# A new issue order for a fused attention and gated-convolution kernel, with q and k of the first batch loaded in alternating halves

## The chip, the cores and the metric

The kernel runs on one core of a Trainium2 chip. The metric is device time in microseconds for one launch. The core has five engines that work from queues of their own, each in order: PE (matrix products into PSUM, eight banks), DVE and ACT (both read PSUM and write SBUF), POOL (elementwise work in SBUF, and the issue of the input loads) and SP (the issue of transposing copies inside SBUF and of the stores). PEld is the loading of weights for PE.

## What is computed

For 8 batches, 8 heads, 576 positions and 64 dimensions a head: attention with an exponential feature map of 2 x 128 features, then a gated convolution over the positions, done with a real Fourier transform of length 576, and a projection out.

```python
def phi(x):
    proj = np.einsum('bhsd,df->bhsf', x, w_phi)
    proj = proj - np.max(np.abs(proj), axis=-1, keepdims=True)
    return np.concatenate([np.exp(proj), np.exp(-proj)], axis=-1)
q_p, k_p = (phi(q), phi(k))
kv = np.einsum('bhsf,bhsd->bhfd', k_p, v)
z = np.sum(k_p, axis=2)
num = np.einsum('bhsf,bhfd->bhsd', q_p, kv)
den = np.einsum('bhsf,bhf->bhs', q_p, z)[..., None] + 1e-06
x = num / den                                   # heads put side by side: 8 x 576 x 512
x1, x2, x3 = np.split(x @ w_proj, 3, axis=-1)
X2 = np.fft.rfft(x2, n=S, axis=1)
H = np.fft.rfft(filter_fft, n=S, axis=0)[None, :, :]
y = x1 * np.fft.irfft(X2 * H, n=S, axis=1) * x3
out = y @ w_out
```

## The kernel before

The program is a table of small steps, the methods of one class, and a text `PLAN` of some 1,480 words that says in which order they are issued. A word is a method with its arguments and, behind an @, the first PSUM bank that it uses: `Pk,0,1@4` is the k projection of batch 0, pair of heads 1, into banks 4 and 5. `run` (L1026) goes through the words from first to last. Each engine takes its own instructions in that order; between engines only data, PSUM banks and the buffers of rings (two, three or four deep, the dictionary `RING`) hold them back. So the order of the words, the banks and the engine named in a word are the schedule.

One batch goes like this; v is a pair of heads (0 to 3), X a half of the heads (0 or 1), m or c a block of 128 columns or rows.

- Loads by POOL: `load` (L554), 576 KB, or `loadh` (L560), one half of it. q and k are then transposed, by SP with `trh` (L566) or, for batch 0, by PE with `pt`, whose result ACT or DVE copies out (`pte`).
- `Pk`, `Qn`, `Pkt`, `Qnt` (L591 to L621) project with `w_phi` on PE; `maxk`, `maxq` and the short `maxkt`, `maxqt` take the absolute maxima on DVE; `ex`, `exkt`, `exqt` are the exponentials on ACT. `Pq` with `Pqt` projects q once more, with the maxima, transposed through `trm`, subtracted in PSUM. `em` and `vs` scale v by the exponential of k's maxima (ACT, then POOL or DVE).
- `KV` and `NE` with `NEt` (L736) are the attention products on PE; `rc`, `xn`, `rct`, `xnt` divide on DVE. The result is x. It is transposed by SP with `trx` (L780) and `trxt`, or by PE with `ptx` (L789) and `ptxt` and a copy.
- `f1` and `f2` (POOL or DVE) fold x, `F` transforms it (PE), `X2` projects the transform with `w_proj`, `Y1` and `m3` multiply by the filter's transform.
- `X1` and `X3` project the transposed x (in the helper `proj`, whose matmuls are L884), `tm` multiplies them; `I` transforms back (for some blocks cut in two steps, `It` and `Is`), `Ie`, `Ip`, `Im` and `ym` (L1002, POOL or DVE) combine; for one block of four, in most batches, `J` and `yj` do it in one.
- `O` multiplies by `w_out` (L1014), `Oe` copies out, `st` (L1020) stores. A block of 128 rows in pairs of batches (`O,b,4`, with `yt`) takes the remainders of two batches.

At the start the kernel also builds the Fourier matrices: `gi_part`, `gi_fr`, `gi_nr` (POOL) make index tables, `cols_f`, `cols_i` (DVE) factors from them, `ang` (ACT or DVE) angles, `frac` (DVE) reduces them, `sin` (ACT) is the sine. The filter comes with `fl_load` (eight pieces) and `fl_loadt` on SP's queue; `fa` (POOL, L491) folds it, `Hd` transforms it on PE, `He` copies it out. `wz` (L312) is two products of zeros on PE whose result nobody reads; `w_load` loads the other weights.

The batches overlap: while PE projects batch b out, batches b+1 to b+3 are in their attention or loading. The plan fixes how they interleave.

Of the kernel before, what the change touches and what calls it, by code (L numbers as in the profile page):

```python
# [1076 lines left out]
```

## Time and profile before

| | us |
|---|---|
| median of 3 runs | 303.11 |
| lowest and highest of them | 302.89, 308.19 |
| the profiled execution, whole | 304.44 |
| its span, first to last instruction | 302.7 |
| PE busy in the span | 275.4 |
| DVE, ACT, POOL busy | 260.4, 225.8, 208.8 |

All times below are from the one profiled execution, in microseconds from the start of its span. A row of the timeline has its start, its length, the engine and line, the operation with output and input, and in brackets the idle time ahead of it with what ended that. Rows of stretches give the busy time of PE, PEld, DVE, ACT and POOL, then the granted PE clock as a share of full speed, the DMA engines' share and GB/s. Rows of waits give the waiting line, what it waited for, and then the sum, the number and the longest of such waits.

### The profile page before, as it was taken

What the parts mean: (1) busy time and instruction counts of PE and PEld (TensorE: products, weight loads), DVE (VectorE), ACT (ScalarE), POOL (GpSimd) and SP (SyncE); (2) the same over time, 40 slices, a digit from 0 to 9 for tenths busy, and PEclk for the clock granted to TensorE, in tenths of its full rate; (3) what the DMA queues carried; (4) which work ended last, traced back from release to release, by engine and by line L of the source; (5) the groups of instructions that cost most, each with busy time, mean ns of one, the idle gap of its engine ahead of it and who ended that gap; (6) DMA issues with size and microseconds to landing.
All of it is one profiled execution on the core that took longest, in us unless ns stands there. A gap on an engine that the chain in (4) does not pass through costs nothing.

```text
span 302.7 us, 10174 instructions
## 1 busy us (share of the span) xinstructions
PE 275.4 (91%) x4287; PEld 201.3 (67%) x4316; DVE 260.4 (86%) x440; ACT 225.8 (75%) x361; POOL 208.8 (69%) x168
## 2 busy tenths in 40 slices
PE   1858689999999999998999969999999999999992
PEld 0627563778667876686768757667588767786761
DVE  8998779799989799989899976789989998887773
ACT  7999887798868887685988657987758997932320
POOL 8119594997985768469998639968768759443550
PEclk9978899999999999999999999999999999999999
DMA  7999999997999859997998966997734342040426
GB/s 135 191 191 185 186 205 170 159 160 119 107 159 202 117 114 155 175 176 119 200 167 151 106 111 106 155 194 118 132 76 69 71 89 64 20 98 2 90 63 196
DMA packets 72446, 40.12 MB, mean 133 GB/s; under 512 B 52752, under 2 KB 67216, under 8 KB 72400
## 3 DMA queue, kind: packets, MB, share of 16 engines
q1 hardware_dynamic: 57184, 22.56, 43.6%
q0 software_dynamic: 14816, 16.25, 35.3%
q8 instruction: 33, 0.54, 0.8%
q10 hardware_dynamic: 400, 0.66, 0.8%
q14 instruction: 13, 0.11, 0.1%
HBM read 33.75 MB, written 9.44 MB: 143 GB/s over the span
## 4 chain that ended last, share of the span: by engine, by line
PE 72%; ACT 9%; DVE 8%; DMA 5%; issue 3%; POOL 2%; SPq 0%; DVEq 0%; ACTq 0%
PE ps L884 17%; PE ps L862 12%; PE ps L1014 9%; PE ps L729 5%; PE ps L937 5%; PE ps L743 4%; DMA xT<-xn 3%; PE ps L603 2%; PE ps L630 2%; DVE mq L672 2%; PE ps L893 2%; PE ps L827 2%; PE ps L596 2%; PE ps L823 2%; PE ps L636 2%
## 5 line engine op out<-in xcount | busy, mean ns | idle before, releaser
L884 PE MATMUL ps<-xT,wproj 128*128 128x256 bf16 x512 | 64.2, 273 | 3.4 <-DMA xT<-xn 3.3
L884 PEld LDWEIGHTS <-wproj 128*128 128x128 bf16 x512 | 48.3, 98 | 13.6 <-issue 4.1
L672 DVE TENSOR_REDUCE mq<-ps 128x8 f32<-128x1024 f32 (+1 forms) x40 | 43.7, 1112 | 5.2 <-PE ps L603 2.5
L672 DVE TENSOR_REDUCE mk<-ps 128x8 f32<-128x1024 f32 (+1 forms) x40 | 44.2, 1112 | 4.6 <-PE ps L596 3.3
L1003 POOL TENSOR_TENSOR yT<-cv,x1s 128x576 bf16<-128x576 f32 x24 | 30.8, 1298 | 18.2 <-DVE x1s L929 9.5
L817 POOL TENSOR_TENSOR xf<-SD 128x512 bf16<-128x512 bf16 x25 | 29.1, 1177 | 14.3 <-DVE SD L811 13.7
L876 POOL TENSOR_TENSOR T<-T,T 128x1024 bf16<-128x1024 bf16 x14 | 29.6, 2122 | 13.2 <-DVE T L872 13.2
L714 POOL TENSOR_TENSOR vp<-vn,vp 128x1152 bf16<-128x1152 bf16 x14 | 30.2, 2154 | 9.0 <-ACT vp L708 9.0
L658 ACT ACTIVATE Eqp<-ps 128x1024 bf16<-128x1024 f32 x32 | 32.6, 1040 | 4.8 <-PE ps L636 4.8
L658 ACT ACTIVATE Eqm<-ps 128x1024 bf16<-128x1024 f32 x32 | 32.7, 1041 | 4.6 <-PE ps L636 4.6
L714 POOL TENSOR_TENSOR vm<-vn,vm 128x1152 bf16<-128x1152 bf16 x16 | 35.1, 2197 | 1.0 <-ACT vm L708 0.7
L658 ACT ACTIVATE Ekp<-ps 128x1024 bf16<-128x1024 f32 x32 | 33.0, 1035 | 2.9 <-PE ps L596 1.9
L1014 PE MATMUL ps<-wout,yT 128*128 128x512 bf16 x132 | 34.1, 380 | 0.9 <-POOL xf L817 0.2
L658 ACT ACTIVATE Ekm<-ps 128x1024 bf16<-128x1024 f32 x32 | 33.1, 1036 | 1.4 <-DVE mk L672 0.9
L862 PE MATMUL ps<-wproj,XF 128*128 128x512 bf16 x119 | 30.0, 380 | 0.6 <-issue 0.2
L811 POOL TENSOR_TENSOR SD<-xn 128x512 bf16<-128x512 bf16 x20 | 23.0, 1171 | 9.2 <-DVE xn L762 7.8
L296 ACT CAST x1s<-ps 128x512 bf16<-128x512 f32 (+1 forms) x32 | 17.9, 560 | 14.9 <-PE ps L884 7.9
L958 DVE TENSOR_TENSOR cv<-es,ps 128x288 f32<-128x288 f32 x52 | 21.2, 445 | 4.0 <-PE ps L862 1.4
L925 DVE TENSOR_TENSOR x1s<-ps,x1s 128x512 bf16<-128x512 f32 x32 | 21.8, 683 | 3.0 <-PE ps L884 2.1
L762 DVE TENSOR_TENSOR xn<-ps,r 128x512 bf16<-128x512 f32 x32 | 21.8, 688 | 1.0
L743 PE MATMUL ps<-KVs,Eqp 128*128 128x65 bf16 x256 | 20.5, 195 | 1.7 <-ACT Eqp L658 0.9
L1014 PEld LDWEIGHTS <-yT 128*128 128x128 bf16 x144 | 12.9, 98 | 13.5 <-POOL yT L1003 0.8
(177 smaller groups left out, 673.5 us busy)
## 6 DMA issues: line engine op xcount, KB each, us to landing
out_dram<-o SPq DMA_DIRECT2D x67, 128.0 KB, 2.6
vn<-in_v_dram POOLq DMA_DIRECT2D x8, 576.0 KB, 6.9
kn<-in_k_dram POOLq DMA_DIRECT2D x7, 576.0 KB, 8.5
qn<-in_q_dram POOLq DMA_DIRECT2D x7, 576.0 KB, 9.6
wproj<-in_moe_w_proj_dram POOLq DMA_DIRECT2D x3, 512.0 KB, 9.8
fl<-in_moe_filter_fft_dram SPq DMA_DIRECT2D x8, 128.0 KB, 6.8
out_dram<-o ACTq DMA_DIRECT2D x5, 128.0 KB, 2.8
...
```

Of the source, the lines that this page charges most:

```text
L658: self.nc.scalar.activation(e, p, AF.Exp, bias=0.0, scale=1.0 if g == "p" else -1.0)
L672: self.nc.vector.tensor_reduce(out=out, in_=src, axis=AX.X, op=ALU.max, apply_absolute_value=True)
L714: self.eng(eng).tensor_tensor(out=t[:, :, :, 0:64], in0=self.at("vn", b)[:, 2 * X:2 * X + 2], in1=t[:, :, :, 64:65].to_broadcast([128, 2, ...
L743: self.mm(self.pb(u, 65 * a, 65 * a + 65), E, KVs[:, u, v, s, :], start=(s == 0), stop=(s == 1))
L762: self.nc.vector.tensor_tensor(out=o, in0=n[:, :, :, 0:64], in1=self.at("r", 4 * b + v).to_broadcast([128, 2, 4, 64]), op=ALU.mult)
L811: self.eng(eng).tensor_tensor(out=o[:, :, 2 * i:2 * i + 2, :], in0=x[:, :, 0:2, :], in1=x[:, :, 2:4, :], op=ALU.subtract if i else ALU.add)
L817: self.eng(eng).tensor_tensor(out=o[:, :, 2 * i:2 * i + 2, :], in0=x[:, :, 0:4:2, :], in1=x[:, :, 1:4:2, :], op=ALU.subtract if i else ALU ...
L862: self.mm(self.pb(0), l, w[:, kt, 512:1024], start=(kt == 0), stop=(kt == 3))
L876: self.eng(eng).tensor_tensor(out=Y, in0=Y, in1=self.at(f"T{2 * e + 1}", b), op=ALU.add)
L884: self.mm(o[:, d], w[:, kt, f0 + 128 * m:f0 + 128 * m + 128], y[:, 1, ::-1, ::-1] if d else y[:, 0], start=(kt == 0), stop=(kt == 3))
L1003: self.eng(eng).tensor_tensor(out=self.at("yT", b)[:, m, 0:SEQ], in0=self.turn_of("cv", (b, m)).rearrange("p x h t -> p (x h t)"), in1=sel ...
L1014: self.mm(self.pb(0), y[:, kt, 128 * c:128 * c + 128], w[:, kt, :], start=(kt == 0), stop=(kt == 3))
```

## The change

Only the text `PLAN` differs; every method is as before. The words are almost the same multiset: 1,484 for 1,483. What differs in kind:

- At the start POOL issues the first halves of q and k, then the second halves (before: q, q, k, k, with the generators in between at other places), then `load,q,1`, `load,v,0`, `load,k,1` (before: `load,k,1`, `load,q,1`, `load,v,0`). The first `loadh` stands ahead of `gi_part`. One of the three first filter loads is put later; four of the other pieces stand between `trh,q,1,0` and `trh,q,1,1`, three behind `trh,k,1,1`.
- `ang,3` goes to ACT and `ang,4` to DVE; one copy `pte` goes from ACT to DVE, `ptxe` of batch 0 wholly to DVE, `gen_neg` to ACT. Eight `wz` instead of nine, with other places and banks.
- `trxt,0` on SP replaces `ptxt,0` on PE; `ptx,3,3` on PE replaces `trx,3,3` on SP; `It` and `Is` replace two `I`.
- Many evacuations (`X1e`, `Fe`, `KVe`, `Oe`, `f1`, `f2`, `m3`, `trme`) change between ACT, DVE and POOL; one `ym` of the last batch goes from POOL to DVE.
- The order of the words, and the banks, differ throughout: `load,q,3` stands ahead of `ym,POOL,0,0`; `trh,q,4,1` stands ahead of `trx,2,0`; `load,q,7` stands behind `load,k,7`.

The lines of the plan in which these stand, out of 163 removed and 163 added:

```diff
-fl_load,2,0 cols_m gi_part fl_load,1,1 loadh,q,0,0 cols_f fl_load,2,1 gi_fr w_load,phi cols_i
-loadh,q,0,1 ang,ACT,1 gi_nr loadh,k,0,1 ang,ACT,4 ang,DVE,3 loadh,k,0,0 load,k,1 ang,ACT,0 gz,DVE
-ident wz,18@0 frac,3 load,q,1 wz,2@1 load,v,0 frac,1 ang,DVE,2 pt,q,0,0,0@0 sin,3 w_phi zeros
...
-ex,k,m,0,3@2 Pq,0,1@6 trh,k,1,1 exkt,m,0@0 w_load,proj,0 Pq,0,3@2 em,p,0,1 em,m,0,1 ex,q,p,0,1@6
-vs,POOL,m,0,1 Qn,1,0@0 fl_loadt KV,0,0@4 ex,q,m,0,1@6 maxq,1,0@0 fl_load,0,1 fl_load,0,0
-ex,q,m,0,3@2 Pq,0,2@6 fl_load,1,0 KVe,DVE,0,0@4 Pk,1,1@0 ex,q,m,0,2@6 vs,POOL,p,0,1 fl_load,3,1
...
-fa,POOL,1 ptx,0,2@7 rc,0,0@0 ex,k,p,1,0@4 NEt,0@2 xn,0,0@0 rct,0@2 ptxe,ACT,0,2@7 ptx,0,0@6
-xnt,0,1@2 ptx,0,3@4 xnt,0,0@2 Pk,1,3@0 ptxe,ACT,0,3@4 ptxe,DVE,0,0@6 fa,POOL,0 Pkt,1@2 Qn,1,2@6
...
-He,ACT,4,0@1 F,0,3@4 vs,POOL,m,1,0 tm,0,3@0 F,0,1@6 Fe,ACT,0,3@4 ptxt,0@1 F,0,0@2 trh,q,2,0
...
-Pq,1,3@4 em,p,2,0 rc,1,1@6 xn,1,1@6 KV,1,1@2 load,q,3 ex,q,m,1,3@4 Im,0,2@0 trx,1,1 vs,POOL,p,2,0
...
-X3,1,3@3 rc,2,0@6 exkt,p,3@4 rc,2,1@0 xn,2,0@6 exkt,m,3@4 X1,1,0@2 xn,2,1@0 trx,2,0 tm,1,3@3
-f1,POOL,2,0,0 Pqt,2@0 maxkt,3@4 KV,2,1@6 trx,2,1 exqt,p,2@0 m3,POOL,1,0 exqt,m,2@0 Pq,2,3@4
...
-F,2,0@0 st,SP,0,2,1 yt,ACT,1 O,1,0@6 ex,k,m,3,0@2 f1,DVE,2,1,0 st,SP,0,0,0 Fe,DVE,2,0@0 trh,q,4,1
...
-X1t,2@1 trx,3,3 Im,2,3@2 J,2,0@6 Ip,2,3@2 X1te,ACT,2@1 tmt,2@0 st,SP,1,2,1 Im,2,2@4 ym,POOL,2,3
...
-ym,POOL,3,1 maxk,5,1@2 exqt,p,4@6 J,3,2@0 st,SP,2,1,1 Ie,3,0@4 st,SP,2,3,1 Im,3,0@4 load,q,7
...
-I,7,1@6 tmt,7@0 tm,7,1@5 Ie,7,1@6 I,7,0@2 ym,POOL,7,3 Ip,7,1@6 Ie,7,0@2 X3,7,2@5 Im,7,1@6
-ym,POOL,7,1 Ip,7,0@2 J,7,2@6 Im,7,0@2 tm,7,2@5 ym,POOL,7,0 O,6,3@2 yj,7,2@6 Oe,ACT,6,3@2 yt,DVE,7
-O,7,1@6 st,SP,6,3,1 O,7,4@7 Oe,ACT,7,1@6 st,SP,6,3,0 O,7,3@2 st,ACT,7,1,0 st,SP,7,1,1 Oe,DVE,7,4@7
-O,7,2@6 st,ACT,7,4,1 st,SP,7,4,0 Oe,DVE,7,3@2 O,7,0@7 st,ACT,7,3,0 st,SP,7,3,1 Oe,DVE,7,2@6
-st,ACT,7,2,1 st,SP,7,2,0 Oe,DVE,7,0@7 st,ACT,7,0,1 st,SP,7,0,0
+fl_load,2,1 cols_m loadh,q,0,0 fl_load,1,1 w_load,phi gi_part gi_fr cols_f loadh,k,0,0 cols_i
+ang,ACT,0 gi_nr ang,ACT,1 loadh,q,0,1 loadh,k,0,1 ang,DVE,4 load,q,1 ang,ACT,3 gz,DVE ident wz,18@0
+load,v,0 one frac,1 pt,q,0,0,1@1 ang,DVE,2 load,k,1 pt,q,0,0,0@0 pte,DVE,q,0,0,1@1 sin,1 frac,3
+wz,2@1 pte,DVE,q,0,0,0@0 pt,k,0,0,0@2 w_phi frac,0 Qn,0,0@0 frac,2 sin,0 Qn,0,1@4 pt,q,0,1,0@3
+sin,3 maxq,0,1@4 pt,k,0,1,1@6 pt,q,0,1,1@7 pte,DVE,q,0,1,0@3 sin,2 maxq,0,0@0 Qn,0,2@4
+pte,ACT,q,0,1,1@7 wz,23@3 pt,k,0,1,0@7 maxq,0,2@4 pt,k,0,0,1@3 pte,ACT,k,0,1,0@7 wz,9@0
...
+maxq,0,3@0 Qnt,0@6 ex,k,m,0,0@4 fl_load,1,0 fl_load,3,1 ex,k,p,0,0@4 maxk,0,1@2 Pk,0,2@0
+fl_load,0,0 ex,k,p,0,2@0 fl_loadt maxqt,0@6 trh,q,1,1 maxk,0,0@4 ex,k,m,0,2@0 Pkt,0@6 ex,k,m,0,1@2
...
+trh,k,1,0 maxk,0,3@4 mhi,0 exkt,m,0@6 wz,28@1 mlo,DVE,0 ex,k,m,0,3@4 vs,DVE,p,0,0 trm,0@0 wz,26@6
...
+em,m,0,1 ex,q,p,0,3@2 Pk,1,1@4 Qn,1,3@0 w_load,proj,1 maxk,1,1@4 ex,q,m,0,3@2 vs,POOL,m,0,1
+KVe,DVE,0,0@6 ex,k,m,1,1@4 Pq,0,2@2 maxq,1,3@0 NE,0,1@6 ex,q,m,0,2@2 w_load,proj,2 rc,0,1@6
+KV,0,1@0 ex,q,p,0,2@2 xn,0,1@6 gen_ends,POOL trx,0,1 ex,k,p,1,1@4 Pq,0,0@2 KVe,DVE,0,1@0 Pk,1,0@6
+ex,q,m,0,0@2 fa,POOL,1 maxk,1,0@6 NE,0,3@0 NE,0,2@4 ex,q,p,0,0@2 rc,0,3@0 xn,0,3@0 ex,k,m,1,0@6
+Pqt,0@2 rc,0,2@4 NE,0,0@0 fa,POOL,0 xn,0,2@4 exqt,p,0@2 rc,0,0@0 exqt,m,0@2 wz,22@4 xn,0,0@0
+ptx,0,2@5 ex,k,p,1,0@6 ptx,0,3@4 ptxe,DVE,0,2@5 Qnt,1@0 NEt,0@2 ptxe,DVE,0,3@4 load,v,1 maxqt,1@0
...
+Hd,0@6 maxq,1,1@2 ex,k,p,1,2@0 X3,0,3@4 trxt,0 vs,POOL,m,1,0 He,ACT,0,0@6 He,DVE,4,0@7 F,0,3@0
...
+em,p,2,0 exkt,m,2@2 I,0,0@0 rc,1,0@4 exkt,p,2@2 xn,1,0@4 NE,1,1@6 Ie,0,0@0 load,q,3 I,0,1@2 trx,1,0
...
+f1,DVE,2,0,1 f1,POOL,2,0,0 Pk,3,1@6 exqt,p,2@0 trh,q,4,1 X3,1,0@4 maxk,3,1@6 exqt,m,2@0
+ex,q,m,2,3@2 NE,2,2@0 f2,POOL,2,0,1 trx,2,0 tm,1,0@4 X2,1,4@5 ex,q,p,2,3@2 rc,2,2@0 xn,2,2@0
...
+tmt,2@1 st,SP,1,1,1 Ip,2,3@4 I,2,2@6 Im,2,3@4 trh,k,5,1 Ie,2,2@6 ptx,3,3@1 ym,POOL,2,3 I,2,1@4
...
+X1e,ACT,4,2@4 X3,4,3@5 X1e,DVE,4,3@2 load,k,7 ex,k,m,5,3@0 f1,DVE,4,1,1 O,3,3@2 load,q,7 rct,4@6
...
+ym,DVE,7,1 X3,7,0@0 st,SP,6,0,1 Im,7,3@6 st,SP,6,2,0 X1,7,2@4 Oe,DVE,6,1@1 ym,POOL,7,3 tm,7,0@0
+X3,7,2@1 st,SP,6,1,0 X1e,ACT,7,2@4 Ip,7,0@2 st,SP,6,1,1 Im,7,0@2 J,7,2@6 tm,7,2@1 ym,POOL,7,0
+O,6,3@1 yj,7,2@6 Oe,ACT,6,3@1 yt,DVE,7 O,7,1@6 st,SP,6,3,1 O,7,4@7 Oe,ACT,7,1@6 st,SP,6,3,0 O,7,3@1
+st,ACT,7,1,1 st,SP,7,1,0 Oe,DVE,7,4@7 O,7,0@6 st,ACT,7,4,1 st,SP,7,4,0 Oe,DVE,7,3@1 O,7,2@7
+st,ACT,7,3,1 st,SP,7,3,0 Oe,DVE,7,0@6 st,ACT,7,0,1 st,SP,7,0,0 Oe,DVE,7,2@7 st,ACT,7,2,1
+st,SP,7,2,0
```

279 lines of the change are left out of this document (136 added, 143 removed).

## The prediction

> **What bounds the kernel now.** I read the page's first part, then the busy time by stretches, then the waits of the matmul engine in the long middle, then the timeline at the three places where it stands still.
>
> ```profile
> span 302.7 us, 10174 instructions
> ## 1 busy us (share of the span) xinstructions
> PE 275.4 (91%) x4287; PEld 201.3 (67%) x4316; DVE 260.4 (86%) x440; ACT 225.8 (75%) x361; POOL 208.8 (69%) x168
> ```
>
> PE is busy 275.4 of 302.7 us, so 27.3 us is all that an order could give back. Where these lie:
>
> ```profile
> core 0: us, PE busy (x) PEld busy (x) DVE busy (x) ACT busy (x) POOL busy (x), PEclk, DMA share, GB/s
> 0.00:10.00 10.00, 3.62 (x26) 2.10 (x28) 8.63 (x54) 8.16 (x14) 7.44 (x21) 1.00 0.86 144
> 10.00:30.00 20.00, 14.91 (x272) 10.50 (x272) 18.91 (x25) 19.78 (x30) 8.19 (x6) 0.83 1.16 190
> 30.00:40.00 10.00, 7.34 (x169) 6.32 (x164) 6.99 (x13) 7.61 (x11) 6.67 (x6) 0.83 1.26 191
> 40.00:290.00 250.00, 242.20 (x3803) 178.68 (x3824) 220.56 (x342) 189.03 (x307) 183.77 (x135) 1.00 0.78 125
> 290.00:302.70 12.70, 7.28 (x40) 3.67 (x39) 5.36 (x10) 1.17 (x2) 2.75 (x3) 0.97 0.45 125
> ```
>
> Up to 40 us PE lacks 6.4 + 5.1 + 2.7 = 14.1 us; from 10 to 30 us ACT (19.78 of 20) and DVE (18.91) are the bound there, not PE and not the loads. From 40 to 290 us PE works 242.20 of 250 and is itself the bound: 7.8 us are lost. The end loses 5.4. Of the 7.8 the trace names these:
>
> ```profile
> PE ps L884 <- DMA xT<-xn: 3.3, 2, 2.4
> PE ps L743 <- issue: 0.8, 1, 0.8
> PE ps L596 <- ACT Eqm L658: 0.6, 1, 0.6
> PE ps L611 <- DVE xnt L774: 0.4, 1, 0.4
> PE ps L603 <- DMA qT<-qn: 0.3, 1, 0.3
> ```
>
> The two at the top are projections of x that wait for a transposed x, once in batch 3 and once in batch 4:
>
> ```profile
> 141.95 1.58 PE L884 MATMUL ps<-xT,wproj 128*128 128x256 bf16 x13 [0.90 <-DMA xT<-xn]
> ...
> 176.34 2.45 PE L884 MATMUL ps<-xT,wproj 128*128 128x256 bf16 x21 [2.40 <-DMA xT<-xn]
> ```
>
> **The change, part by part.** The matmuls are the same but for trifles: one warming pair `wz` fewer, `ptx,3,3` (four transposes on PE) for `trx,3,3`, `trxt,0` for `ptxt,0` (two off PE), `It`+`Is` for two `I`. I set their sum to zero: a PE second counts only past 40 us, and there four transposes come against two. So the time can move only through waits: at the head, in the middle, at the end.
>
> *Head, start.* POOL now issues the first half of q ahead of `gi_part`, on which DVE's `cols_f` and so ACT's first `ang` wait:
>
> ```profile
> 1.40 0.88 POOL L561 DMA_DIRECT2D qn<-in_q_dram  x1 [0.23 <-issue]
> ```
>
> That issue is 0.88 us, and 0.23 of idle just ahead of it may hide part, so the generators start 0.6 to 0.9 us later; I take 0.6, since the queue's own start-up hides some too. `gi_fr` keeps one load ahead of it, as before. ACT gets `ang,3` (three wide operations) for `ang,4` (two wide), +0.6, and loses one of three transposed-input copies, -0.65:
>
> ```profile
> L420 ACT ACTIVATE turn<-fr,cols 128x288 f32<-128x288 f32 x4 | 2.2, 613 | 0.0
> ```
>
> ```profile
> L296 ACT COPY kT<-ps 128x640 bf16<-128x640 bf16 (+1 forms) x2 | 1.2, 642 | 0.0
> ```
>
> DVE takes that copy (0.44) and, with a third `maxq` of 1.2 ahead of the copy of the first k, brings that k about as late as ACT comes free; `frac,4` and one `ang` go out of its way.
>
> ```profile
> L298 DVE COPY qT<-ps 128x512 bf16<-128x512 bf16 (+1 forms) x3 | 1.3, 440 | 0.1
> ```
>
> ```profile
> L672 DVE TENSOR_REDUCE mq<-ps 128x8 f32<-128x1024 f32 x3 | 3.6, 1214 | 0.0
> ```
>
> The first exponential, now here:
>
> ```profile
> 15.32 1.02 ACT L658 ACTIVATE Ekp<-ps 128x1024 bf16<-128x1024 f32 x1
> ```
>
> comes 0.6 us later, and because ACT has next to no gaps to 30 us, it stays 0.6 later. The order of the loads itself (v of batch 0 ahead of k of batch 1, `load,q,1` earlier, four filter loads between the transposes of q and k of batch 1) I cost at nothing: no engine is short of these bytes between 10 and 30 us, ACT's and DVE's work is the cover, and if it were gone, POOL's `fa` would be the first to be late, since it waits for the last filter load now:
>
> ```profile
> POOL fs L492 <- DMA fl<-in_moe_filter_fft_dram: 3.3, 1, 3.3
> ```
>
> Behind `fa` on POOL stand `load,v,1`, `load,k,2` and the first `f1`. A wait of up to 3.3 there is what POOL bears today without PE waiting for it by name, so it adds nothing.
>
> *Head, end.* Before, the first projection follows this:
>
> ```profile
> 37.68 0.69 DVE L762 TENSOR_TENSOR xn<-ps,r 128x512 bf16<-128x512 f32 x1
> 39.37 0.21 DVE L768 RECIPROCAL rt<-ps 128x8 f32<-128x8 f32 x1 [0.99 <-PE ps L752]
> 39.61 0.86 DVE L774 TENSOR_TENSOR xnt<-ps,rt 64x256 bf16<-64x256 f32 x2
> 40.39 0.41 DVE L298 COPY xT<-ps 128x512 bf16<-128x512 bf16 x1
> ```
>
> ```profile
> 41.25 0.76 PE ps L884 x6
> ```
>
> so 2.9 us after the last `xn` of batch 0 ends (38.37). After the change `rct` and both `xnt` stand behind, and DVE makes all three copies of 0.41 and one short maximum (about half of 1.2): 1.8 us of DVE work plus the transposes' hand-over, so 2.0. Gain 0.9. The head is then 0.6 - 0.9 = -0.3. Its bounds: this stretch also holds a stall inside one group of `Pq` matmuls,
>
> ```profile
> 31.47 1.49 issue
> ```
>
> which may or may not come again (-1.8), and upwards the 0.9 of the late start with no gain at the end (+0.9).
>
> Also, one warming pair fewer (eight for nine) meets a PE whose clock falls to a half in the head:
>
> ```profile
> 20.00:22.50 2.50, 1.27 (x6) 0.57 (x5) 2.50 (x4) 2.33 (x7) 0.83 (x2) 0.50 1.01 151
> 22.50:25.00 2.50, 2.50 (x28) 1.55 (x28) 2.50 (x2) 2.50 (x7) 2.36 (x3) 0.50 1.10 209
> ```
>
> With a second such stretch of 5 us PE would do half its work in it: at most 2.5 us, less what ACT's bound hides. I put that into the upper bound of the head, +0.9 + 2.5 = +3.4, not into the sum. The Trainium skill (TensorE: Matmul & The Clock Gate, section "What's actually happening") holds that one idle window of some 3.4 us halves PE's clock and a busy one restores it; that speaks against fewer warming matmuls, and by it the time would be 302.8. The trace agrees with its half, 0.50 in both rows.
>
> *Batch 3.* `trx,3,3` leaves SP's queue; PE transposes and ACT copies (0.59, ACT is at 76% in the middle). Three SP transposes remain and the last of them hangs on an earlier `xn`; the wait of 0.90 goes. -0.9, between 0 and -0.9; what is late next there is PE itself.
>
> *Batch 4.* The transposed x landed 5.82 us after its issue, with a 576 KB load of q issued into it:
>
> ```profile
> 170.48 5.82 DMA xT<-xn
> ```
>
> ```profile
> 171.83 0.81 POOL L555 DMA_DIRECT2D qn<-in_q_dram  x1
> ```
>
> ```profile
> DMA to landing us min/median/max: 3.8/4.4/5.8
> ```
>
> That load (`load,q,7`) is moved on POOL behind two `ym` and an `f2`, so past this wait, and one of two stores between the transposes goes. With the median of the four transposes there, 4.4, the wait shrinks by 1.4; with 3.8 by 2.0, with 5.8 by nothing. I take -1.4.
>
> *Batch 3's q.* `load,q,3` moves on POOL ahead of `ym,0,0`, where POOL waits for DVE; its transposes then come earlier and the 0.3 on L603 goes: -0.3 (0 to -0.3).
>
> *End.* The last product waits for POOL:
>
> ```profile
> PEld L1014 <- POOL yT L1003: 0.5, 1, 0.5
> ```
>
> ```profile
> 288.95 3.84 POOL L1003 TENSOR_TENSOR yT<-cv,x1s 128x576 bf16<-128x576 f32 x3 [3.87 <-DVE x1s L929]
> ```
>
> Three `ym` on POOL, 1.28 each; one of them goes to DVE, so POOL is done before the last `J` and the wait goes: -0.5. The last five products, their copies and stores keep their order but for one swap.
>
> *New waits.* The changed places in SP's and POOL's queues can make a wait of the kind seen: their median in the list above is 0.6. I add one: +0.6.
>
> Sum: -0.3 - 0.9 - 1.4 - 0.3 - 0.5 + 0.6 = -2.8. The profiled execution took 304.44 us (302.7 of span, 1.74 around it), 1.3 above the median of the runs, 303.11; the difference is put on the median: **300.3 us**. With the bounds (all gains at their least, the head at +3.4 and three new waits, +5.2; all at their most, -5.5) this case by itself runs from 297.6 to 308.3.
>
> **The rivals.** *Slower: x comes late in the middle.* SP is one queue. Before, `trx,2,0` and `trx,2,1` are issued ahead of a transpose of batch 4; now `trh,q,4,1` stands ahead of all four `trx,2`, and it waits for a load of 576 KB and for the last reader of q of batch 2. Behind it on SP are the four transposes of x, and on those hang PE's projections. The `trx` of batches 1, 3 and 4 share that queue with stores and transposes in new places. If each of these four batches pays what batch 4 pays now, that is 4 x 2.4 = 9.6 in place of 3.3, +6.3: 309.4. It decides once the last transpose lands later than PE has filler, and batch 4 shows that 5.8 us is too late. For it: batches 3 and 4 wait already, so the cover is thin. Against it: batches 1 and 2 do not, and in the new order no fewer groups of matmuls stand between a batch's last `NE` and its first projection. Chance 0.24.
>
> *Faster by more.* All named waits of the middle go (5.4 in the list), and the end's 0.5, and the head's 0.3: -6.2, 296.9. For it: each is tied to a place in the order; against it: L743's 0.8 is "issue", which no order shows. Chance 0.19.
>
> *Nothing happens.* What is gained at one place is waited for at the next, PE work being equal: 303.1. Chance 0.12. That leaves 0.45 for the forecast.
>
> **How the numbers follow.** The bound of 2%, about what a measurement of this kernel can tell from no change, lies at 297.0 and 309.2. The forecast and the third rival end within it but for their edges; the faster rival lies on its edge and gets 0.19 beyond; the slower one sits at its edge with its spread upwards, 0.26 with the forecast's own tail. Within: 0.55. The range goes from 296.0 (the faster rival with a little more) to 310.0 (the slower one with one more wait); some 0.05 is left out below and 0.13 above.
>
> **What would show it.** Right: the wait of L884 on xT below 2 us in total; the first exponential near 15.9 and the first L884 near 41; PE busy within 1 us of 275.4; no wait of L1014 on POOL at the end. Wrong: a wait of L884, L596 or L603 on a DMA of over 2 us in batches 1, 2 or 5; `fs` on POOL waiting for its load longer than 3.3; PEclk at 0.5 for a stretch past 25 us; or DVE above 90% in the middle, with PE waiting for its maxima.

## The result, and the profile after

| | before | after |
|---|---|---|
| median, us | 303.0 (302.75 to 308.19) | 312.45 (311.17 to 312.9) |
| after / before | | 1.031, 95% 1.027 to 1.035 |
| span of the profiled execution | 302.7 | 308.4 |

The change is slower by 3.1%; 300.3 was forecast, with a range to 310.0. Some executions of a kernel come out in a slower state, over 1.5% above its fastest: the medians here and below are over all of them, the ratios over the others alone. The profiled execution of the changed kernel took 311.17, the least of its four.

First the page of the changed kernel, its span and its first part:

```profile
span 308.4 us, 10199 instructions
## 1 busy us (share of the span) xinstructions
PE 278.4 (90%) x4316; PEld 201.3 (65%) x4316; DVE 268.0 (87%) x446; ACT 223.2 (72%) x359; POOL 204.3 (66%) x164
```

PE is busy 3.0 longer than before (29 of its records were missing there) and idle 2.7 longer. The stretches of before, once more, for the changed kernel:

```profile
0.00:10.00 10.00, 2.26 (x12) 1.39 (x13) 7.35 (x49) 6.55 (x11) 7.24 (x21) 1.00 0.79 119
10.00:30.00 20.00, 14.14 (x232) 8.88 (x231) 17.88 (x26) 19.20 (x31) 6.38 (x5) 0.83 1.20 191
30.00:40.00 10.00, 5.84 (x152) 5.29 (x152) 7.94 (x10) 6.17 (x8) 7.89 (x6) 0.83 1.15 206
40.00:290.00 250.00, 242.83 (x3837) 177.57 (x3837) 223.57 (x344) 188.30 (x307) 179.14 (x132) 0.99 0.73 122
```

Up to 40 PE is 3.6 less busy than before (2.26 + 14.14 + 5.84 = 22.2 for 25.9), so the head is late by about that. In the long middle PE is as busy as before, but at a clock of 0.99, and the waits are others. PE's waits, and two groups of the page:

```profile
PE ps L743 <- DVE KVs L298: 2.7, 1, 2.7
PE ps L729 <- issue: 2.3, 1, 2.3
PE ps L823 <- DVE mq L672: 2.3, 2, 1.8
...
PE ps L743 <- issue: 1.0, 1, 1.0
```

```profile
L884 PE MATMUL ps<-xT,wproj 128*128 128x256 bf16 x512 | 63.8, 273 | 0.1
...
L1014 PE MATMUL ps<-wout,yT 128*128 128x512 bf16 x144 | 36.1, 387 | 0.0
```

What the change was forecast to remove is gone: L884's 3.3 of waiting for transposed x is 0.1, and L1014 no longer waits for POOL. In its place stand 2.7 and 2.3 for DVE, and 3.3 of "issue", idle time behind which the profile shows no semaphore. The chain of waits passes through all of them:

```profile
20.08 6.97 DMA flt<-in_moe_filter_fft_dram
...
29.32 0.23 DVE turn L452
29.55 2.48 issue
...
77.93 0.55 PE ps L729 x27
78.48 2.33 issue
80.80 0.90 PE ps L729 x44
...
182.80 0.89 DVE xf L817
183.69 2.85 issue
186.54 1.82 DVE mq L672 x2
...
200.91 0.82 PE ps L743 x23
201.73 0.96 issue
```

Two of the "issue" pieces follow a DVE operation, two stand between two matmuls of one word of the plan (L729 is the sum over k and v, `KV`, L743 the numerators, `NE`). They have different causes. The timelines of the changed kernel's DVE, POOL and ACT show the first kind; DVE:

```profile
27.08 1.11 DVE L298 CAST f<-flt 64x512 bf16<-64x512 f32 x1 [1.34 <-DMA flt<-in_moe_filter_fft_dram]
28.11 1.21 DVE L672 TENSOR_REDUCE mq<-ps 128x8 f32<-128x1024 f32 x1
29.25 2.86 DVE L452 TENSOR_SCALAR turn<-turn 128x576 int32<-128x576 int32 x1
...
182.72 3.89 DVE L817 TENSOR_TENSOR xf<-SD 128x512 bf16<-128x512 bf16 x1
```

POOL:

```profile
1.25 0.88 POOL L561 DMA_DIRECT2D qn<-in_q_dram  x1 [0.80 <-POOLq L1061]
2.23 0.15 POOL L321 IOTA part<- 128x1 int32 x1
...
29.41 2.18 POOL L714 TENSOR_TENSOR vm<-vn,vm 128x1152 bf16<-128x1152 bf16 x1
...
181.94 2.29 POOL L817 TENSOR_TENSOR xf<-SD 128x512 bf16<-128x512 bf16 x2
184.17 2.16 POOL L714 TENSOR_TENSOR vp<-vn,vp 128x1152 bf16<-128x1152 bf16 x1
```

ACT:

```profile
17.33 1.02 ACT L658 ACTIVATE Ekm<-ps 128x1024 bf16<-128x1024 f32 x1
```

Each of the two long DVE operations ends just after a POOL operation on SBUF (29.41 + 2.18 = 31.59 beside 32.11; 184.17 + 2.16 = 186.33 beside 186.61). Where POOL is idle the same forms take 0.45 and 0.41. `TENSOR_REDUCE`, which reads PSUM, keeps its 1.2 beside POOL. The start is late as well: `part` at 2.23 (0.84 before), the first exponential at 17.33 (15.32 before).

### The profile page after: what moved, and what is told of

It reads as the page before. It is cut to its first block, busy times and chain, and to the rows that moved or that the text cites. A ratio compares the mean times of both kernels' runs of the same rounds, so it can differ in the third digit from the quotient of the medians.

```text
span 308.4 us, 10199 instructions
## 1 busy us (share of the span) xinstructions
PE 278.4 (90%) x4316; PEld 201.3 (65%) x4316; DVE 268.0 (87%) x446; ACT 223.2 (72%) x359; POOL 204.3 (66%) x164
## 4 chain that ended last, share of the span: by engine, by line
PE 71%; DMA 9%; DVE 9%; issue 4%; SPq 2%; POOL 2%; ACT 1%; DVEq 0%; POOLq 0%; ACTq 0%
PE ps L884 15%; PE ps L862 11%; PE ps L1014 8%; PE ps L729 5%; PE ps L937 5%; PE ps L743 5%; DMA out_dram<-o 4%; DMA qn<-in_q_dram 3%; DVE mq L672 3%; PE ps L993 2%; PE ps L630 2%; PE ps L893 2%; DMA flt<-in_moe_filter_fft_dram 2%; PE ps L823 2%; PE ps L827 2%
## 5 line engine op out<-in xcount | busy, mean ns | idle before, releaser
L884 PE MATMUL ps<-xT,wproj 128*128 128x256 bf16 x512 | 63.8, 273 | 0.1
L884 PEld LDWEIGHTS <-wproj 128*128 128x128 bf16 x512 | 48.5, 98 | 10.8
L714 POOL TENSOR_TENSOR vm<-vn,vm 128x1152 bf16<-128x1152 bf16 x14 | 30.9, 2212 | 19.1 <-ACT vm L708 19.0
L714 POOL TENSOR_TENSOR vp<-vn,vp 128x1152 bf16<-128x1152 bf16 x15 | 32.2, 2149 | 14.8 <-ACT vp L708 14.8
L1003 POOL TENSOR_TENSOR yT<-cv,x1s 128x576 bf16<-128x576 f32 x25 | 31.7, 1281 | 14.6 <-DVE cv L958 10.5
L1014 PE MATMUL ps<-wout,yT 128*128 128x512 bf16 x144 | 36.1, 387 | 0.0
L296 ACT CAST x1s<-ps 128x512 bf16<-128x512 f32 (+1 forms) x30 | 15.8, 533 | 16.9 <-PE ps L884 6.9
L811 POOL TENSOR_TENSOR SD<-xn 128x512 bf16<-128x512 bf16 x17 | 19.9, 1179 | 10.4 <-DVE xn L762 10.3
L872 DVE TENSOR_TENSOR T<-ps,HTo 128x1024 bf16<-128x1024 f32 x16 | 19.3, 1219 | 4.6 <-PE ps L862 4.5
L743 PE MATMUL ps<-KVs,Eqp 128*128 128x65 bf16 x256 | 19.7, 192 | 2.9 <-DVE KVs L298 2.7
```

Of the source, the lines that this page charges most:

```text
L714: self.eng(eng).tensor_tensor(out=t[:, :, :, 0:64], in0=self.at("vn", b)[:, 2 * X:2 * X + 2], in1=t[:, :, :, 64:65].to_broadcast([128, 2, ...
L743: self.mm(self.pb(u, 65 * a, 65 * a + 65), E, KVs[:, u, v, s, :], start=(s == 0), stop=(s == 1))
L884: self.mm(o[:, d], w[:, kt, f0 + 128 * m:f0 + 128 * m + 128], y[:, 1, ::-1, ::-1] if d else y[:, 0], start=(kt == 0), stop=(kt == 3))
L1003: self.eng(eng).tensor_tensor(out=self.at("yT", b)[:, m, 0:SEQ], in0=self.turn_of("cv", (b, m)).rearrange("p x h t -> p (x h t)"), in1=sel ...
L1014: self.mm(self.pb(0), y[:, kt, 128 * c:128 * c + 128], w[:, kt, :], start=(kt == 0), stop=(kt == 3))
```

## The experiments

Eighteen runs; e8_order, with two executions, is told with e12_order. "Against the changed kernel" is the start of the same matmuls in the two profiled executions; it shows where a difference arises. An idle time of PE is counted as the profile does, from the end of the last matmul; the expectations count some of them from its start, which gives about 0.2 more. The times:

| run | median, us | before beside it | ratio, 95% |
|---|---|---|---|
| e1_start (one of four at 693.3) | 313.95 | 304.79 | 1.026 (1.007 to 1.045) |
| e2_frac4 | 311.30 | 304.79 | 1.024 (1.010 to 1.037) |
| e3_ft | 311.02 | 304.79 | 1.026 (1.017 to 1.035) |
| e4_f2 | 309.62 | 304.79 | 1.020 (1.009 to 1.031) |
| e5_all | 311.13 | 303.37 | 1.026 (1.019 to 1.034) |
| e6_loads | 311.47 | 303.37 | 1.026 (1.014 to 1.038) |
| e7_six | 306.86 | 303.37 | 1.013 (1.005 to 1.020) |
| e9_q3 | 317.17 | 304.14 | 1.044 (1.037 to 1.051) |
| e10_bshift | 306.01 | 304.14 | 1.005 (1.000 to 1.010) |
| e11_best | 312.48 | 304.14 | 1.021 (1.014 to 1.028) |
| e12_order | 303.75 | 304.14 | 0.995 (0.991 to 0.9995) |
| e13_shift | 306.67 | 304.06 | 1.010 (1.006 to 1.015) |
| e14_comb | 306.94 | 304.06 | 1.010 (1.006 to 1.014) |
| e15_hold | 305.07 | 304.06 | 1.000 (0.995 to 1.004) |
| e16_beat | 303.50 | 304.06 | 1.001 (0.997 to 1.004) |
| e17_same | 311.53 | 304.25 | 1.024 (1.019 to 1.030) |
| e18_f2shift | 304.03 | 304.25 | 1.002 (0.998 to 1.006) |

Two bounds on what these can show. The changed kernel itself is at 1.031 and, in e17_same, at 1.024. The intervals of the four single edits (e1_start to e4_f2) all reach into 1.024 to 1.031, so none of their times shows a gain, and what is said of them is read from the traces. And e17_same is a second profile of the same kernel: it is level with the first within 0.1 up to 77, 0.6 ahead at 79 (an idle time of 1.70 for 2.33), 2.6 ahead at 192 (the clock falls at 202.0 and not at 188.7) and 0.6 behind at 206 (2.86 idle for 0.96, and the clock). So a lead of that size behind such a place is not the edit's by itself.

### One part undone at a time

e1_start:

```diff
-fl_load,2,1 cols_m loadh,q,0,0 fl_load,1,1 w_load,phi gi_part gi_fr
+fl_load,2,1 cols_m fl_load,1,1 w_load,phi gi_part loadh,q,0,0 gi_fr
```

> The changed kernel with one word moved: the load of the first half of q goes back behind the two iotas of gi_part on POOL. Theory A (the late start is the loss): part is written at 0.84 again instead of 2.23, the first exponential comes at about 16 instead of 17.33, and 1.3 to 2.0 us reach the end: 310.5 to 311.2 against 312.45. Theory B (the start is covered, the loss is made later, where vector work on SBUF is held behind POOL): the first exponential comes earlier all the same, but the time stays within 0.7 of 312.45, since the transfers and the held turn<-turn near 29 stand where they stood. Theory C (order of loads itself): time gets worse, because the first half of q lands later.

PE was 1.0 to 1.8 ahead of the changed kernel from 11 to 81, and the first exponential came at 16.12 for 17.33, so far as Theory A has it. The 1.3 to 2.0 that were to reach the end did not: PE was 0.3 ahead at 84 and 2.4 behind at 210, after idle time and falls of the clock near 80 and 200; e17_same shows the like near 200 without an edit.

e2_frac4:

```diff
-Qn,0,0@0 frac,2 sin,0
+Qn,0,0@0 frac,2 frac,4 sin,0
...
-w_load,proj,0 frac,4 fl_load,3,0
+w_load,proj,0 fl_load,3,0
```

> The changed kernel with frac,4 moved from behind the loads of the projection to directly behind frac,2, where POOL has nothing on SBUF. Theory B (DVE is held behind POOL's vs): the 128x576 turn<-turn takes 0.4 to 0.45 instead of 2.86, the mask maximum behind it and ACT's mask exponential come 2.4 earlier, TensorE's idle time between 30 and 40 falls from 4.2 to about 2, and 1.5 to 3 us reach the end: 309.5 to 311. Rival (the 2.86 lies beside a wait that would be there anyway, for instance the late start or the transfers): 312.45 within 0.7.

e3_ft:

```diff
-Pq,0,1@4 ft,DVE vs,POOL,p,0,1
+Pq,0,1@4 vs,POOL,p,0,1
...
-Pq,0,3@2 maxq,1,0@0 fl_load,2,0
+Pq,0,3@2 maxq,1,0@0 ft,DVE fl_load,2,0
```

> The changed kernel with the cast of the half-size filter rows (ft on DVE) moved one step back, behind the maximum maxq,1,0. The 1.34 that DVE waits for the transfer of flt near 27 goes, the cast itself stays beside POOL's vs. If that wait is one of the terms: 0.8 to 1.5 less, 311 to 311.7. If the turn<-turn behind it is held by POOL until POOL's vs ends at 31.6 whatever comes before (Theory B taken strictly), nothing: the turn<-turn takes the more, and the time stays at 312.45 within 0.5.

In both the 2.86 was gone and PE was 3.1 and 3.3 ahead at 37; in e3_ft because `frac,4` now fell into a gap of POOL's work. Of that, 1.4 and 1.9 were left at 45 (in e2_frac4 0.6 from 49): the first L884 waited 1.5 and 2.0 for transposed x of batch 0. So the held operation is a cause of the late head, with a transfer close behind it. What it costs at the end is not shown: 1.024 and 1.026 are no gain, and in the profiled executions PE is 1.5 behind and 0.6 ahead at 300.

e4_f2:

```diff
-X1e,ACT,4,0@3 f2,DVE,4,1,0 trxt,4 Pk,5,2@6 f2,POOL,4,0,1
+X1e,ACT,4,0@3 trxt,4 Pk,5,2@6 f2,POOL,4,0,1 f2,POOL,4,1,0
```

> The changed kernel with one of the four xf<-SD products of batch 4 moved from DVE to POOL, behind POOL's own three. Theory B: the 3.89 us product on DVE at 182.7 is gone, the maxima of batch 5 come about 3.5 earlier, TensorE's 2.28 idle between 180 and 190 falls below 0.6, and with the granted clock of 0.90 to 0.93 in 180 to 200 back at 1.0 the kernel gains 2 to 4 us: 308.5 to 310.5. Rival (the maxima are late because of their own inputs, or POOL becomes late and holds vs of batch 5): within 0.7 of 312.45, with the idle time turned up at the next vs or mask step.

DVE's timeline of e4_f2 (lines lie 3 lower there): the maxima start at 183.31 for 186.54, and ACT is what they wait for.

```profile
183.31 1.82 DVE L669 TENSOR_REDUCE mq<-ps 128x4 f32<-128x512 f32 x2 [1.24 <-ACT o L293]
```

PE is 0.4 ahead before the wait and 3.0 at 188, so 2.6 is the wait of 2.3 with what hangs on it. It is 3.9 ahead at 190 and 4.6 at 192, because the clock no longer falls. In the changed kernel it falls to 0.50 behind that wait:

```profile
188.70:192.10 3.40, 3.40 (x18) 2.04 (x17) 2.85 (x4) 2.04 (x7) 2.21 (x1) 0.50 1.25 182
```

That part can't be put down to the edit: in e17_same, with the held product in place, the clock didn't fall there either. At 197 2.5 of the 4.6 go again in an idle time without a semaphore, 3.48 instead of 0.96 (e17_same has 2.86 there).

### Together, and the loads

e5_all is the four edits at once.

> The four single edits together: the load of q's first half back behind gi_part, frac,4 behind frac,2, ft behind maxq,1,0, one xf<-SD product of batch 4 on POOL. Alone they moved TensorE at equal work by -1.4 (start), -3.1 and -3.3 (near 37, of which -1.0 and -1.9 were left at 45, where the first L884 then waited 1.5 to 2.0 for a transposed xT of batch 0), and -4.0 (near 190). Theory B (held vector work) with the start: -1.4 and -1.9 at 45, -4.0 at 190, the sum -6 to -7 at 190: 305 to 307. Rival (they share one cover, the transposes and fetches of instructions, so that each takes only what the other leaves): -4 in all, 308 to 309.

Both theories expected a lower time than 1.026; the rival came nearer: PE is 3.2 ahead at 45 with nothing left at 84, and 3.7 ahead at 192 with 1.5 left at 203. Both times idle time without a semaphore had grown (2.54 for 2.33 and 3.21 for 0.96), and that became the question.

The traces have the transfers that bring PE's instructions: 33 or 34 of 16 KB. All these stalls stand in PE's program a multiple of 256 instructions apart (weight loads counted, up to a few that a trace lacks), also where the program was shifted by 128 (e13_shift), and PE goes on 1.3 to 1.5 after such a transfer ends. Worked out from the traces' transfers and PE's instructions, in us; "entered" is where PE began the 256 instructions ahead of the stall:

```
run          block entered  transfer starts, ends  PE's last start, goes on
after             74.4          78.0   79.4          78.3   80.8
after            199.0         200.5  201.4         201.5  202.7
e17_same          74.4          77.5   78.8          78.3   80.2
e17_same         196.4         199.7  200.6         198.9  202.0
e4_f2            194.5         198.3  199.2         197.0  200.6
e6_loads          98.6         103.2  104.2         102.9  105.5
e9_q3             74.2          76.1   77.3          78.1   78.6
e9_q3            198.8         202.2  203.1         201.3  204.6
e13_shift         76.3          79.9   81.0          80.6   82.5
```

So a block is probably asked for about when the one before it is entered. In these rows PE goes on 3.6 to 6.9 after that (199.0 to 202.7, 98.6 to 105.5), and where it runs a block in less, as the small matmuls of `KV` and `NE` do (2.5 from 199.0, 3.9 from 74.4), the rest is a stall.

e6_loads:

```diff
-load,v,3 X2,0,2@1 ex,q,m,1,0@6
+X2,0,2@1 ex,q,m,1,0@6
...
-f1,POOL,1,1,0 O,0,3@0
+f1,POOL,1,1,0 load,v,3 O,0,3@0
...
-load,v,7 st,SP,3,4,1
+st,SP,3,4,1
...
-m3,POOL,4,1 KVe,ACT,5,1@0
+m3,POOL,4,1 load,v,7 KVe,ACT,5,1@0
```

> The changed kernel with two loads of v later on POOL's queue: v of batch 3 from 63.6 to about 81 (behind the product f1,POOL,1,1,0), v of batch 7 from 195.3 to about 204 (behind m3,POOL,4,1). Theory D (TensorE runs out of instructions, and their fetch waits behind a DMA that is filled by loads): the load of q of batch 3 lands some 3 us earlier, the 16 KB fetch that starts at 77.8 starts earlier, and the 2.3 idle in the middle of KV,2,0 and the 1.0 near 201 go: -2 to -3, 309.5 to 310.5. Rival (the fetch is asked for late by the place in the instruction stream, whatever the DMA does): both stalls stay, 312.45 within 0.7.

A miss by the choice of loads: 1.70 idle stayed at 78, as much as e17_same has without an edit; q of batch 3 was still in flight. A stall of 2.37 came new at 103.

e9_q3:

```diff
-load,v,3 X2,0,2@1 ex,q,m,1,0@6
+load,q,3 X2,0,2@1 ex,q,m,1,0@6
...
-Ie,0,0@0 load,q,3 I,0,1@2
+Ie,0,0@0 I,0,1@2
...
-f1,POOL,2,0,0 Pk,3,1@6
+f1,POOL,2,0,0 load,v,3 Pk,3,1@6
```

> The changed kernel with q of batch 3 loaded where v of batch 3 was (63.6 instead of 71.9) and v of batch 3 at about 104 (behind f1,POOL,2,0,0), so that no load is in flight from about 73 to 79. Theory D (a fetch of 256 TensorE instructions waits while a 576 KB load is in flight; TensorE goes on some 1.4 after it ends): the fetch that started at 77.8, 3.7 after its block of 256 was entered near 74.1, starts near 75.5, and the 2.3 idle in KV,2,0 goes or is below 0.4: -2 to -2.5 at 81, about 310 at the end. Rival (the place in the stream alone): the stall stays near 2, no gain.

The chain of e9_q3 at both places:

```profile
77.78 0.55 PE ps L729 x27
78.33 0.31 issue
78.64 0.90 PE ps L729 x41
...
200.68 0.82 PE ps L743 x23
201.50 3.05 issue
```

The transfer at 76.1 starts 1.9 after the block is entered, not 3.7, and 2.33 shrinks to 0.31. Now q of batch 3 lands at 76.3, just behind the transfer's start; in the changed kernel it lands at 80.9, behind the start at 78.0. That speaks for Theory D at this place. The other transfers of the changed kernel go with it: where a load of POOL's was in flight when the block ahead was entered, they start 1.0 to 4.1 after that (16 of them, median 2.2), and where none was, between 0.7 ahead of it and 1.2 after (17, median 0.6). That is an association and not a test.

The whole is slower all the same: at 201 the stall is 3.05, and 2.4 was lost at 121, where PE waited 2.2 for what DVE does behind one more long product. With the loads moved, it lies beside POOL's `vs` (DVE's and POOL's timelines of e9_q3; in the changed kernel the DVE row takes 0.68):

```profile
118.39 3.15 DVE L817 TENSOR_TENSOR xf<-SD 128x512 bf16<-128x512 bf16 x1
```

```profile
119.08 2.17 POOL L714 TENSOR_TENSOR vm<-vn,vm 128x1152 bf16<-128x1152 bf16 x1
```

e7_six is e5_all with e6_loads' edits and the one below; e11_best has e9_q3's loads for e6_loads'.

```diff
-Qn,1,3@0 w_load,proj,1 maxk,1,1@4
+Qn,1,3@0 maxk,1,1@4
...
-load,k,2 Pk,1,3@0
+load,k,2 w_load,proj,1 Pk,1,3@0
```

> The four single edits and the two later loads of v, and the second third of the projection loaded behind k of batch 2 instead of beside the filter rows (it is what the transpose of batch 0's xT waits behind near 40, by Theory D). If all terms are apart: 5.5 to 6.5 of the four, 2 to 3 of the loads, 1.5 of the transpose, together 302 to 304, on a level with the kernel before. If the stalls for instructions only move to the next dense stretch: 305 to 307.

> The changed kernel with the four single edits, the second third of the projection behind k of batch 2, and q of batch 3 ahead of v of batch 3 as in e9_q3. If the terms are apart: -2 to -2.5 at 45, -4 to -4.5 at 81, -7 to -8 at 190: 304 to 305, near the kernel before but not ahead of it. If the stall of 200 grows as in the run with the four edits (3.4 instead of 1.15): 306 to 307.

e7_six came nearest so far, 2.6 ahead at 82, but lost 3.4 from 84 to 99, where the load of v moved to 81 is in flight with others; its 306.86 lies in the 305 to 307 of "the stalls only move". In e11_best's profiled execution 4.6 at 37 was lost by 57 (4.13 of waiting for ACT's `Ekp` at 55), and the clock was 0.71 in 50 to 60; at 315.69 it lies above the median of 312.48, so this may be of that execution alone. Neither says more of the cause.

### The order of the loads by itself

e8_order and e12_order are the same kernel: before, with the changed kernel's order of loads.

```diff
-fl_load,2,0 cols_m gi_part fl_load,1,1 loadh,q,0,0 cols_f fl_load,2,1 gi_fr w_load,phi cols_i
-loadh,q,0,1 ang,ACT,1 gi_nr loadh,k,0,1 ang,ACT,4 ang,DVE,3 loadh,k,0,0 load,k,1 ang,ACT,0 gz,DVE
-ident wz,18@0 frac,3 load,q,1 wz,2@1 load,v,0 frac,1
+fl_load,2,0 cols_m loadh,q,0,0 gi_part fl_load,1,1 cols_f fl_load,2,1 gi_fr loadh,k,0,0 w_load,phi
+cols_i ang,ACT,1 gi_nr loadh,q,0,1 loadh,k,0,1 load,q,1 ang,ACT,4 ang,DVE,3 ang,ACT,0 gz,DVE ident
+wz,18@0 frac,3 wz,2@1 load,v,0 load,k,1 frac,1
```

> The kernel before, with the loads at its head put into the order of the changed kernel and nothing else: the first half of q ahead of the iotas, the halves in turn (q, k, q, k), then q of batch 1, v of batch 0, k of batch 1. Theory A (the order of loads is the loss): 304.5 to 306, the first exponential 1.4 to 2 late and the delay kept to the end. Theory B (the loss lies in what was searched anew around it): the first exponential comes late by 1.4 at most, and at the end the time is within 1 of 303.0. The prediction had put the head at -0.3.

> The kernel before with only the order of its loads changed, once more and in more rounds, since one round gave 301.9 and 309.3. Theory A (the order of loads is the loss): 1.005 to 1.01 of the time of before. Theory B: 0.998 to 1.004.

e8_order gave 301.89 and 309.25, which decides nothing. e12_order is at 0.995 of before: the order of loads that names the change isn't the loss. The profiled execution of e12_order took 310.94, far above its median, so the head is better read from e16_beat below, which has the same order of loads at its head (302.72): the first exponential comes 1.4 late there (16.74), PE is 1.7 late at 11, 0.3 at 38 and level at 41.

### The held operation in the other kernel

e15_hold, on the kernel before:

```diff
-sin,0 frac,4 Qn,0,1@0
+sin,0 Qn,0,1@0
...
-KVe,DVE,0,0@4 Pk,1,1@0
+KVe,DVE,0,0@4 frac,4 Pk,1,1@0
```

> The kernel before with one word moved: frac,4 from behind sin,0 (where POOL is idle, 0.45) to behind the first KVs copy (KVe,DVE,0,0), where POOL's vs of 27.2 to 29.4 runs. Theory B: the turn<-turn takes 1.8 to 2.5 there, the mask maximum behind it comes as much later, and 0.5 to 2 us reach 41; with a fall of the clock after it up to 1.7 more: 303.8 to 306. Rival (the length beside POOL is the profile's own doing): 0.45 there, or a long one with no later mask maximum, 303.0 within 0.7.

DVE's and POOL's timelines of e15_hold:

```profile
27.43 2.34 DVE L452 TENSOR_SCALAR turn<-turn 128x576 int32<-128x576 int32 x1
29.70 1.21 DVE L672 TENSOR_REDUCE mk<-ps 128x8 f32<-128x1024 f32 x1
```

```profile
27.32 2.14 POOL L714 TENSOR_TENSOR vp<-vn,vp 128x1152 bf16<-128x1152 bf16 x1
```

Held for 2.34 instead of 0.45, and PE 2.1 late at 29, but 0.3 at 38, level at 41, and at the end nothing that the comparison resolves (1.000, 0.995 to 1.004); the 303.8 to 306 that Theory B expected did not come. So the operation is held in both kernels, and how much of it reaches the end depends on the work behind it.

### Moving the borders of the blocks

e10_bshift is before with 64 PE instructions more (`wn,18` for `wz,20` and `wz,22`), e13_shift the changed kernel with 128 more, as in the diff: `wn` issues small matmuls on zeros where `wz` issued two large ones.

```diff
+    def wn(self, i):
+        z = self.at("zz")
+        for _ in range(i):
+            self.mm(self.pb(0, 0, 65, 0, 64), z[:, 0:64], z[:, 0:65], True, True)
...
-exkt,m,0@6 wz,28@1 mlo,DVE,0
+exkt,m,0@6 wn,34@1 mlo,DVE,0
...
-trm,0@0 wz,26@6
+trm,0@0 wn,34@6
```

> The kernel before, with two pairs of filler matmuls at 21 to 23 replaced by 18 small ones each: 64 more TensorE instructions (weight loads counted), with no more work to speak of, so that the borders of the blocks of 256 instructions come 64 earlier in every later stage. By the trace of before, blocks of 256 would then be run in 4.0 (ending at 75), 3.0 (167), 2.4 (195) and 3.1 (230), against 3.6 or more that a fetch took there from border to going on. Theory D: idle without a semaphore of about 0.5 to 1.5 at each of 167, 195 and 230, in all 2 to 4.5 more: 305 to 307.5. Rival (fetches are no cause): 303.0 within 0.8.

> The changed kernel with two pairs of filler matmuls (wz,28 and wz,26) replaced by 34 small ones each: 128 more TensorE instructions, so that the blocks of 256 begin 128 earlier in the program. Theory D: the block that ends at 200 is then run in 4.8 instead of 2.6 and its stall of 1.15 (up to 3.4 in other runs) goes; the one at 78 stays near 2, moved by 128 instructions, because the load of q of batch 3 is still in flight; a new one of up to 0.5 near 135: -0.5 to -2, 310.5 to 312. Rival (stalls belong to the place in the program): idle at the same KV and NE matmuls as before, 312.45 within 0.7.

e10_bshift: idle of 1.4 at 168 is new, as expected; at 195 it is 1.1, little more than the 0.8 of before; none came at 75 and 230, and 0.8 at 138 and 1.0 at 202 were not expected. The time, 1.005, lies below the expectation: borders move the stalls, but where and how long can't be told from how long the blocks take alone. e13_shift: the waits of PE for "issue" (line numbers are 5 higher there) have moved from `KV` at 78 to the output products behind it, and the one near 200 is gone; the other is near 39.

```profile
PE ps L1019 <- issue: 1.5, 1, 1.5
PE ps L748 <- issue: 1.2, 1, 1.2
```

The gain is more than expected, 1.031 or 1.024 to 1.010. It isn't the blocks' alone: the small fillers take longer than the large ones, and behind them `frac,4` falls into a gap of POOL's, so its 2.4 is gone too (DVE's timeline of e13_shift):

```profile
29.73 0.45 DVE L457 TENSOR_SCALAR turn<-turn 128x576 int32<-128x576 int32 x1
```

Of the 2.0 that this made PE earlier at 37, 0.1 was left at 45, behind the new stall of 1.2 near 39. The lead is 3.5 at 203: about 0.7 from the stall of 78 (2.4 ahead at 79, but 0.7 at 84, behind the 1.5), 1.1 from the stall at 201, and 1.7 because the clock does not fall at 188.7, which it doesn't in e17_same either, without an edit. So the stalls are half of it.

### Terms together

e14_comb is e5_all with e9_q3's loads and e13_shift's fillers. e16_beat is e12_order with this:

```diff
-NE,4,2@0 st,SP,2,0,1 f2,POOL,4,0,0 tmt,3@6 Pk,5,1@2
-st,SP,2,2,1 rc,4,2@0
+NE,4,2@0 f2,POOL,4,0,0 tmt,3@6 Pk,5,1@2
+rc,4,2@0
...
-trx,4,3 Pqt,4@6
+trx,4,3 st,SP,2,0,1 st,SP,2,2,1 Pqt,4@6
...
-Im,3,0@4 load,q,7
+Im,3,0@4
...
-load,k,7 maxq,5,1@0
+load,k,7 load,q,7 maxq,5,1@0
```

> The changed kernel with the four single edits, q of batch 3 ahead of v of batch 3, and the shift by 128 instructions. If late start, held vector work and instruction fetches are the whole of the loss: -1.6 to -2.3 at 45, -4 at 81, -8 at 190, -9 at 203, and with no fall of the clock after 40 the time of before or 1 less, 302 to 304.5. If other waits take their place: 306 to 309, and the windows show which.

> The kernel before with the order of loads of e12_order (0.995 of before) and, in batch 4, the two stores that stand ahead of the last x transposes moved behind them and the load of q of batch 7 moved behind the load of k of batch 7. If the 2.4 that TensorE waits near 174 for a transposed x is those two: 1.5 to 2.4 less than e12_order, 299.5 to 301 where before is at 303, 0.987 to 0.99. If the transposes are late by their own time or the later load makes batch 7's q late: 0.995 to 1.0.

e14_comb is no better than the shift alone: what the other edits give is taken by something else. What, isn't known: in its profiled execution one transpose of k took 12.9 near 117, and PE waited 5.5 for it, but that execution took 316.23, far above the median of 306.94. e16_beat was 2.1 ahead of before at 176, so the wait of batch 4 can be had alone. In the profiled executions 1.9 was left at 188 and 1.5 at 290 (the stall near 194 is 1.12 for 0.78), but the ratio of 1.001 shows none of it, nor the 0.5% of e12_order.

e17_same is the changed kernel, e18_f2shift the shift with e4_f2's edit.

> The changed kernel as it is, once more, on the chip of the next run. If the first comparison holds: 1.027 to 1.035 of before. If e13_shift was low because of its chip: 1.01 to 1.02.

> The changed kernel with the shift by 128 instructions and the product f2 of batch 4 on POOL. If the two terms are apart: e13_shift less 2.3 to 4, that is 1.000 to 1.003 of before. If something else takes the place of the held product: 1.008 to 1.012, as e13_shift.

On another chip the changed kernel is slower as well: 1.024 (1.019 to 1.030), a little under the 1.027 to 1.035 expected and above the rival's 1.01 to 1.02. The two edits of e18_f2shift bring the kernel level with before. From e13_shift to e18_f2shift it is 0.8%, some 2.4, beside the 2.6 that the edit of e4_f2 gave at 188. Stretches of before, of after and of e18_f2shift around the head, the first stall and batches 4 and 5:

```profile
28.00:42.00 14.00, 9.67 (x214) 8.14 (x211) 10.08 (x19) 11.58 (x15) 10.68 (x9) 0.88 1.24 198
74.00:86.00 12.00, 11.95 (x212) 8.93 (x211) 11.09 (x19) 9.69 (x17) 10.15 (x10) 1.00 1.12 118
180.00:206.00 26.00, 24.96 (x431) 17.98 (x434) 20.36 (x36) 21.80 (x34) 22.03 (x16) 1.00 0.93 146
```

The changed kernel:

```profile
28.00:42.00 14.00, 9.20 (x264) 8.09 (x259) 11.87 (x16) 10.17 (x14) 11.89 (x10) 0.87 1.01 181
74.00:86.00 12.00, 9.67 (x249) 7.08 (x246) 8.24 (x15) 8.39 (x12) 8.18 (x7) 1.00 1.09 147
180.00:206.00 26.00, 22.76 (x373) 15.41 (x371) 20.67 (x29) 18.62 (x31) 14.69 (x10) 0.93 0.84 134
```

e18_f2shift:

```profile
28.00:42.00 14.00, 10.28 (x320) 9.00 (x316) 11.57 (x19) 13.45 (x16) 13.33 (x12) 1.00 1.07 173
74.00:86.00 12.00, 10.67 (x218) 7.18 (x211) 8.99 (x16) 8.81 (x15) 9.82 (x9) 1.00 0.87 125
180.00:206.00 26.00, 25.28 (x451) 18.30 (x449) 21.22 (x35) 22.86 (x37) 20.01 (x14) 1.00 0.90 151
```

PE's busy time in the three is 46.6, 41.6 and 46.2 together, and the changed kernel's clock of 0.93 in the last is 1.00 again.

The clock takes a part in all of this. Over the whole span its mean is 0.966 to 0.977 in the ten executions of the changed kernel on record (0.973 in the mean), 0.978 to 0.992 in those of before that lie within 1.5% of its fastest (0.984) and 0.975 to 0.989 in those of e18_f2shift (0.984). The difference of 0.011, times some 308, is 3.4 of the 7 to 9 between the kernels at most (an estimate, as if PE worked through all of it).

## Why the prediction was wrong

- *Batch 4, batch 3, the end: right.* -1.4, -0.9 and -0.5 were forecast. L884's 3.3 of waits went to 0.1, more than the 2.3 forecast, and L1014's wait for POOL is gone. It did not go only because PE came later: e18_f2shift takes the time of before, and PE waits 0.4 there for transposed x.
- *The slower rival: wrong mechanism.* It came out slower, but no transposed x was late in batches 1 to 4 of the changed kernel; the rival's 309.4 was near the time by chance.
- *"The order of the loads itself ... I cost at nothing": right* (e12_order, 0.995), and so was the late start's small price by itself. The size of the late start was off: `part` was 1.4 late and the first exponential 2.0, not 0.6, since the whole 0.88 of the issue and 0.80 of idle (0.39 in before) stand ahead of `part`, and 0.6 more came behind it, where ACT waited 0.53 at 15.33 for PE's transposes of k. With that one word back, the first exponential comes at 16.12 (e1_start).
- *The head, -0.3, is the first step that failed.* "`frac,4` and one `ang` go out of its way" looked at the place that `frac,4` leaves, not at the one it comes to, beside POOL's `vs`: 2.86 for 0.45. `ft` ahead of `maxq,1,0` and behind a late transfer wasn't costed. By 56 PE had done 3.2 less than before (37.7 busy for 40.9), inside the head's bound of +3.4, whose larger part, +2.5, had been given to the clock; up to 40 the clock is 0.87 in both kernels. The first L884 came at 44.1, where 41 was forecast. How much of this reaches the end isn't shown: e2_frac4, e3_ft and e5_all took most of it away at 37 without a gain in time.
- *The second step: no term for DVE work on SBUF beside POOL.* The trace of before could have shown it: its operations lengthened in the same way came to 1.3, 1.1 and 1.0 in three places. In the change one, of 3.89 for 0.41, stands right ahead of the maxima that batch 5 waits for. Taken away it is worth 2.6 at 188 (e4_f2), and 0.8% from e13_shift to e18_f2shift.
- *The third step: "issue, which no order shows".* The 0.8 of L743 and the 1.49 at 31.47 were on the page and were taken as fixed. Every order of PE's words moves the borders of its blocks of 256, so a new plan draws these stalls anew: 2.33 and 0.96 here, 1.70 and 2.86 in the same kernel's second profile, up to 3.48 in other runs.
- *"New waits +0.6"* stood for all of this and was far too small: by the two edits of e18_f2shift it is 1.024 or 1.031 to 1.002, 7 to 9 us, in which the fuller clock is counted.

How the shift's part divides among stalls, clock and `frac,4` isn't settled, since e13_shift removed a little of each; nor whether the clock falls by the order or by chance, since one kernel has it at 188.7 in one execution and at 202.0 in the next; nor why e9_q3 lost more than its trace's 1.9 at 203. That a transfer of instructions waits for loads in flight rests on one place (e9_q3 against the changed kernel) and on the association over the 33 transfers; which queue it waits in was not tried. No version of the changed kernel beat before; e12_order, before with its order of loads, is ahead by 0.5% (0.05 to 0.9%), which e16_beat with the same order (1.001) does not bear out.
